# A fifth transpose for the twin rows of four tiles, a VectorE copy for the first K part, and a reversed wait list

## The chip, the cores and the metric

The kernel runs on one core of one Trainium2 chip. The metric is device time in microseconds (us) of one launch, as the median over several executions. A profiled execution gives, besides, a span (first to last recorded instruction) and a trace of every instruction.

## What is computed

A block of 2048 tokens with width 448 is normalised (layer norm without weights), then goes two ways that are multiplied and added back to the input:

```python
xn = layernorm(x)                               # x: 2048 x 448, bf16
# A: linear attention, 16 heads of 28
q, k, v = split(xn @ wqkv)
phi = lambda t: where(t > 0, t + 1, exp(t)) + 1e-6
kv = einsum("hsd,hse->hde", phi(k), v);  z = phi(k).sum over s
s = (phi(q) @ kv / (phi(q) @ z + 1e-6)) @ wo
# B: dense layer with a squared relu
h = relu(xn @ w1 + b1) ** 2                     # width 1792
g = silu(h @ w2 + b2)
out = x + s * g
```

## The kernel before, in words

**Tiles.** The tokens are cut into 16 tiles of 128 (`si`), four tiles make a group (`g`). For every tile VectorE takes the statistics (L465, L466), ScalarE makes the reciprocal deviation with a Ln and an Exp (L475, L479), and VectorE writes the normalised tile `xn` (L488). The products with `wqkv` and `w1` contract over the 448 columns, so `xn` has to be transposed into `xT`: three full chunks of 128 columns, and a rest of 64 columns.

**The rest and its twin.** The fourth chunk of `xT` holds the rest twice: rows 0 to 63 and rows 64 to 127 are the same 64 columns. The matmuls of the rest use 64 rows only, and two of them, one on each half of the array, run side by side (`half[0]`, `half[1]`). So both halves need the data. Before the change the twin is made ahead of the transpose: for tiles 0 to 3 `ln_last` (L508 to L519) writes the 64 normalised columns twice into `xn[:, si, 384:512]` with one VectorE instruction on an input that is read twice, and a transpose of 128 columns then gives both halves. From tile 4 on a small copy (`ln_twin`, L503) doubles the columns and a DMA makes the whole transpose (L551).

**The head.** Tiles 0 to 3 are transposed by TensorE instead (`pe_transpose`, L521 to L546). Tiles 0 and 1 go in two parts: part 0 is chunks 0 and 1, part 1 is chunks 2 and 3. Tiles 2 and 3 go in one part of four chunks. All transposes of a part land in one PSUM bank (`b`) and are copied to `xT` by the engine that `turn` names. Of part 0 of tile 0 each chunk has its own copy, so that the first K matmul can start after the first (`xT00a`). TensorE's order in the head is the order of the calls in L1069 to L1109: eight matmuls that only warm the array, the transposes `turn(0,0)`, `turn(0,1)`, `turn(1,0)`, then the K product of tile 0 in three parts (`mains(k0, ...)`), `turn(1,1)`, the K product of tile 1, the first halves of four `h` tiles (`h_mains`, 256 tokens), between them the transposes of tiles 2 and 3, and the rests (`rests`, 64-row matmuls). After that come the streams of K, Q and h matmuls of all groups (`pe_four`, `quads`), the products with `w2` (L957), the attention's folding, and the finish (L993, L1002) with the stores.

**What sets the order.** TensorE and the queue on SyncE keep the order in which the operations were added. For VectorE, ScalarE and GpSimd a planner in `schedule` (L88 to L229) chooses by planned durations; in the head two lists written out by hand (L1110 to L1117) fix the order on VectorE and ScalarE. PSUM banks are given out by the planner too. `emit` (L231 to L287) then works out for each operation which semaphores it must see. It goes through the operations that this one depends on from the one that the planner ends last to the one that it ends first, leaves out what is already implied, and keeps the list in that order (L258 to L268); L275 and L276 issue the waits in the order of the list.

```python
            for d in sorted(deps, key=lambda d: -d.end):
...
                need.append((d.sem, d.seq))
...
            waits[op] = need
```

In the built program an instruction holds one wait itself. Where the list has more, the instruction holds the first of the list, and the others stand ahead of it as wait instructions of their own, with one or two waits each; the trace calls these EVENT_SEMAPHORE, at L276.

Of the kernel before, what the change touches and what calls it, by code (L numbers as in the profile page):

```python
# [9 lines left out]
P = 128  # L10
# [45 lines left out]
class Program:  # L56
# [174 lines left out]
    def emit(self, nc, es):  # L231
        sems = {e: es.enter_context(nc.semaphore("q_" + e)) for e in self.ENGINES}
        clock = {}
        count = dict.fromkeys(self.ENGINES, 0)
        n_dma = 0
        last = {o for o in self.ops if o.nbytes and o.writes[0][0] == "out" and not o.succ}
        landed = es.enter_context(nc.semaphore("landed"))
        for e in self.ENGINES:
            k = 0
            for op in self.order[e]:  # L240
                if op in last:
                    op.sem, op.seq, op.key = landed, 16, ("out", op)
                elif op.nbytes:
                    op.sem, op.seq, op.key = es.enter_context(nc.semaphore(f"d{n_dma}")), 16, ("d", n_dma)
                    n_dma += 1
                else:
                    k += 1
                    op.sem, op.seq, op.key = sems[e], k, e
        done = {}
        waits = {}  # L250
        prev = {}
        for op in sorted(self.ops, key=lambda o: (o.start, 0 if o.eng == "pe" else 1)):
            e = op.eng
            known = dict(prev.get(e, {}))
            need = []
            deps = set(op.deps) | set(self.bankdeps.get(op, ()))
            deps.discard(op)
            for d in sorted(deps, key=lambda d: -d.end):  # L258
                if d.key == e == "pe" and d not in op.sync:
                    continue  # L260
                if known.get(d.key, 0) >= d.seq:
                    continue
                need.append((d.sem, d.seq))
                for kk, vv in done[d].items():
                    if known.get(kk, 0) < vv:
                        known[kk] = vv
                known[d.key] = max(known.get(d.key, 0), d.seq)
            waits[op] = need  # L268
            prev[e] = known
            done[op] = known  # L270

        def body_of(e):
            def body(h):
                for op in self.order[e]:
                    for s, v in waits[op]:  # L275
                        h.wait_ge(s, v)  # L276
                    op.emit(h, e).then_inc(op.sem, 16 if op.nbytes else 1)
                if e == "sp":
                    h.wait_ge(landed, 16 * len(last))

            return body

        body_of("pool")(nc.gpsimd)
        body_of("sp")(nc.sync)
        body_of("act")(nc.scalar)
        body_of("pe")(nc.tensor)
        body_of("dve")(nc.vector)  # L287


def bass_recurrent_scan__linear_attn_block__dense_activation_squared_relu__prompt_kernel(  # L290
# [4 lines left out]
    with ExitStack() as es:  # L295
# [186 lines left out]
            )  # L482

        def ln_norm(si, part=None):
            c = (slice(0, D if si > 3 else 384), slice(0, 256), slice(256, 384))[0 if part is None else part + 1]
            return add(
                "dve",
                lambda e, _: e.tensor_scalar(  # L488
                    out=xn[:, si, c], in0=x_tok[:, si, c], scalar1=mv[:, si, 0:1],
                    scalar2=rstd[:, si : si + 1], op0=ALU.subtract, op1=ALU.mult,  # L490
                ),
                [("x", si), ("mv", si), ("rstd", si)], [("xn", si) if part is None else ("xn", si, part)],
                0.4 if part is None else (0.22, 0.18)[part],
            )

        xn_of = lambda si: [("xn", si, 0), ("xn", si, 1)] if si < 2 else [("xn", si)]
# [8 lines left out]
                0.1 + 0.03 * (hi - lo) if eng == "dve" else 0.4,  # L505
            )

        def ln_last(si):  # L508

            x = x_tok[:, si, 384:448]  # L510
            x = bass.AP(tensor=x.tensor, offset=x.offset, ap=[x.ap[0], [0, 2], x.ap[1]])
            return add(
                "dve",
                lambda e, _: e.tensor_scalar(
                    out=xn[:, si, 384:512].rearrange("p (i c) -> p i c", i=2), in0=x, scalar1=mv[:, si, 0:1],
                    scalar2=rstd[:, si : si + 1], op0=ALU.subtract, op1=ALU.mult,
                ),
                [("x", si), ("mv", si), ("rstd", si)], [("xd", si)], 0.18,
            )  # L519

        def pe_transpose(si, part, eng):  # L521


            b = Buf("T")
            chunks = range(4) if part is None else (2 * part, 2 * part + 1)
            for i, c in enumerate(chunks):
                reads = xn_of(si)[c // 2 :][:1] or xn_of(si) if c < 3 else [("xd", si)]
                add(
                    "pe",
                    lambda e, _, i=i, c=c: e.transpose(  # L530
                        ps(b)[:, i * 64 : (i + 1) * 64].bitcast(bf), xn[:, si, c * P : (c + 1) * P], ident[:, :]
                    ),
                    reads + ["ident"] + ([b] if i else []), [b], 0.1,
                )
            def ev(e, _, lo=0, n=len(chunks)):
                src = ps(b)[:, lo * 64 : (lo + n) * 64].bitcast(bf).rearrange("p (c k) -> p c k", c=n)
                dst = xT[:, chunks[0] + lo : chunks[0] + lo + n, si * P : (si + 1) * P]
                if eng == "dve":
                    return e.tensor_copy(dst, src)
                return e.activation(out=dst, in_=src, func=AF.Copy)  # L540

            names = [("xT", si, j) for j in ((0, 1) if part is None else (part,))]
            if (si, part) == (0, 0):
                head["xT00a"] = add(eng, lambda e, x: ev(e, x, 0, 1), [b], [("xT", 0, "a")], 0.25)
                return add(eng, lambda e, x: ev(e, x, 1, 1), [b], names, 0.25)
            return add(eng, ev, [b], names, (0.42 if eng == "dve" else 0.6) if part is None else 0.25 if eng == "dve" else 0.35)  # L546

# [168 lines left out]
        def token_sum(c):  # L716

            b = Buf("A")

            def f(e, _):  # L720
                last = None
                for si in range(NT):
                    if c < 3:
                        last = e.matmul(  # L724
                            ps(b)[:, 0:D], xn[:, si, c * P : (c + 1) * P], pk_of(si), start=(si == 0),
                            stop=(si == NT - 1),
                        )
                    else:
                        r = slice(64 * (si % 2), 64 * (si % 2) + 64)
                        last = e.matmul(  # L730
                            ps(b)[r, 0:D], xn[:, si, 384:448], pk_of(si), start=(si < 2), stop=(si >= NT - 2)
                        )
                return last

            add(
                "pe", f, [("pk", i) for i in range(NT)] + [n for i in range(NT) for n in xn_of(i) + [("xd", i)]], [b], (16 if c < 3 else 8) * MM(D) + 0.1
            )

            def ev(e, eng):
                if eng == "dve":  # L740
                    return e.tensor_copy(at[:, c, :], ps(b)[:, 0:D])
                return e.activation(out=at[:, c, :], in_=ps(b)[:, 0:D], func=AF.Copy)

            add("dve", ev, [b], [("at", c)], 0.63, alts=[("act", 0.55)])
# [304 lines left out]
        for i in range(4):  # L1049
            head[f"st{i}"], head[f"mv{i}"] = ln_stats(i)  # L1050
            head[f"ln{i}"], head[f"ex{i}"] = ln_rstd(i, i + 1)
            for j in (0, 1) if i < 2 else (None,):
                head[f"xn{i}" + ("" if j is None else str(j))] = ln_norm(i, j)
            twin = head[f"xd{i}"] = ln_last(i)
        for op in masks:
            op.after = [twin]

        def warm(n, wide=False, after=()):
            b = Buf("W")
# [14 lines left out]
        def turn(si, part, eng):  # L1074
            head[f"xT{si}{part}"] = pe_transpose(si, part, eng)
# [4 lines left out]

        turn(0, 0, "act")
        turn(0, 1, "act")
        turn(1, 0, "act")
        mains(k0, (0,), [("xT", 0, "a")] + wnames("wk")[:1])
        mains(k0, (1,), [("xT", 0, 0)])
        mains(k0, (2,), [("xT", 0, 1)])
        turn(1, 1, "act")
        mains(k1, (0, 1), [("xT", 1, 0)] + wnames("wk")[:1])
        h_mains(0, (0, 1))
        mains(k1, (2,), [("xT", 1, 1)])  # L1090
# [5 lines left out]
        )  # L1096
        h_mains(0, (2,))
        h_mains(1)
        h_mains(2)
        head["xT2"] = pe_transpose(2, None, "act")  # L1100
        h_mains(3)
        head["xT3"] = pe_transpose(3, None, "dve")
        n = len(pr.ops)
        rests(k0, k1)
        k0.out()
# [2 lines left out]
        rests(first[0], first[2])  # L1108
        rests(first[1], first[3])  # L1109
        for eng, names in (  # L1110
            ("dve", "st0 mv0 st1 mv1 xn00 xn01 xd0 xn10 xn11 xd1 st2 mv2 st3 mv3 xd2 xn2 xd3 xn3 xT3"),
            ("act", "ln0 ex0 ln1 ex1 xT00a xT00 xT01 xT10 xT11 ln2 ex2 ln3 ex3 b1 xT2"),
        ):
            ops = [head[n] for n in names.split()]
            for i, op in enumerate(ops):
# [132 lines left out]
```

## Time and profile before

| | |
|---|---|
| median of 4 runs | 141.27 us (141.20 to 141.64) |
| the profiled execution | 141.34 us, span 139.70 us |
| TensorE matmuls | 136.4 us busy, 98% of the span |
| VectorE, ScalarE, GpSimd busy | 92.3, 77.9, 25.0 us |
| head: first transpose on TensorE | 4.31 us from the span's start |
| head: transposes on TensorE (L530) | 16 |
| head: last of the rests starts | 9.07 us |

The time of a run is longer than the span by 1.64 us in the profiled execution; this is start and end that no instruction covers. In the rows below, a row of the timeline gives start, duration, engine, line, operation, output and inputs; for a matmul the array shape that it uses stands ahead of the operand's shape (`128*128` is the whole array, `64*128` one of two row halves, `128*64` one of two column halves). Matmuls overlap: a row's duration is longer than the distance to the next.

### The profile page before, as it was taken

To read this page: it belongs to the slowest core of one execution; us is meant where nothing else is said; L and a number is where in the kernel's file an instruction comes from. 1 tells how busy PE (TensorE), PEld (TensorE's weight loads), DVE (VectorE), ACT (ScalarE), POOL (GpSimd) and SP (SyncE) were. 2 spreads that over 40 slices of the span, in tenths; PEclk is the share of its full clock that TensorE was granted. 3 is DMA by queue.
4 is the path that set the end of the run, shared out by engine and by line. 5 is a ranking of instruction groups with operands and counts; after the bars stand their busy time and mean duration, and the time that the engine had idled before them with its cause. 6 is when DMAs were issued, how large, how long until landed. Compare 5 with 4: busy or idle time off the path is not lost.

```text
span 139.7 us, 3098 instructions
## 1 busy us (share of the span) xinstructions
PE 136.4 (98%) x1255; PEld 68.1 (49%) x1255; DVE 92.3 (66%) x226; ACT 77.9 (56%) x152; POOL 25.0 (18%) x33
## 2 busy tenths in 40 slices
PE   9899999999999999999999999999999999999993
PEld 2474444444444444444455455645555555555482
DVE  3989889798878995889995900219836072452743
ACT  4769787869988888979788912513033030300220
POOL 6000000000000000000893000000001429092670
PEclk9999999999999999999999999999999999999999
DMA  6996379999722300000000048960000102112132
GB/s 193 242 344 202 55 188 179 359 288 151 130 52 56 66 14 0 0 19 5 0 0 0 33 114 180 175 110 0 0 0 5 66 0 99 37 62 70 37 99 66
DMA packets 20353, 12.90 MB, mean 92 GB/s; under 512 B 9524, under 2 KB 19956, under 8 KB 20340
## 3 DMA queue, kind: packets, MB, share of 16 engines
q1 hardware_dynamic: 18332, 11.52, 33.4%
q10 hardware_dynamic: 2008, 1.20, 4.4%
q8 instruction: 10, 0.16, 0.5%
q14 instruction: 3, 0.02, 0.1%
HBM read 8.78 MB, written 2.10 MB: 78 GB/s over the span
## 4 chain that ended last, share of the span: by engine, by line
PE 95%; DMA 2%; DVE 2%; issue 0%; DVEq 0%
PE pb L957 31%; PE pb L690 30%; PE pb L643 9%; PE pb L1023 8%; PE pb L724 7%; PE pb L674 6%; DMA x_tok<-in_A_x_dram 2%; PE pb L730 1%; PE pb L530 1%; DVE st L465 1%; PE pb L817 1%; PE pb L778 1%; PE pb L855 0%; DVE xn L993 0%; DVE mv L466 0%; PE pb L848 0%
## 5 line engine op out<-in xcount | busy, mean ns | idle before, releaser
L690 PE MATMUL pb<-xT,w 64*128 64x512 bf16 (+2 forms) x408 | 51.6, 365 | 0.0
L957 PE MATMUL pb<-w,r 64*128 64x448 bf16 (+3 forms) x406 | 44.9, 343 | 0.0
L699 ACT ACTIVATE r<-pb,b1f 128x512 bf16<-128x512 f32 x56 | 35.2, 689 | 4.1 <-PE pb L690 4.1
L690 PEld LDWEIGHTS pb<-xT,w 64*128 64x128 bf16 (+1 forms) x408 | 22.8, 94 | 22.5 <-ACT r L699 0.5
L957 PEld LDWEIGHTS pb<-w,r 64*128 64x128 bf16 (+1 forms) x406 | 22.9, 95 | 19.8 <-issue 0.7
L968 DVE TENSOR_TENSOR gbuf<-pb,b2b 128x448 bf16<-128x448 f32 (+1 forms) x16 | 9.2, 608 | 29.7 <-PE pb L957 29.7
L933 ACT ACTIVATE gbuf<-gbuf 128x448 bf16<-128x448 bf16 (+1 forms) x16 | 8.7, 565 | 36.0 <-DVE gbuf L968 35.5
L1002 POOL TENSOR_TENSOR xn<-xn,x_tok 128x448 bf16<-128x448 bf16 x15 | 15.1, 1034 | 46.3 <-DVE xn L993 46.3
L643 PE MATMUL pb<-w_qkv,xT 64*128 64x512 bf16 (+1 forms) x106 | 17.8, 376 | 0.0
L674 PE MATMUL pb<-xT,w_qkv 64*128 64x512 bf16 x84 | 15.5, 376 | 0.0
L707 DVE TENSOR_TENSOR r<-r 128x512 bf16<-128x512 bf16 x42 | 14.4, 416 | 0.0
L392 POOL MEMSET kvm<- 128x2048 bf16 x1 | 1.8, 1805 | 63.6 <-DVE zb L668 63.6
L1023 PE MATMUL pb<-msb,pqT 64*128 64x448 bf16 (+3 forms) x93 | 10.9, 343 | 0.0
L465 DVE BATCH_NORM_STATS2 st<-x_tok 128x6 f32<-128x448 bf16 x16 | 9.3, 609 | 2.3 <-DMA x_tok<-in_A_x_dram 2.3
L631 DVE SCALAR_TENSOR_TENSOR qk<-pb,qk 128x512 bf16<-128x512 f32 x16 | 10.6, 684 | 0.2
L993 DVE TENSOR_TENSOR xn<-pb,gbuf 128x448 bf16<-128x448 f32 (+2 forms) x17 | 9.2, 590 | 2.0 <-ACT gbuf L933 1.5
L621 ACT ACTIVATE qk<-pb 128x512 bf16<-128x512 f32 x16 | 8.9, 593 | 3.0 <-PE pb L643 2.4
L643 PEld LDWEIGHTS pb<-w_qkv,xT 64*128 64x128 bf16 (+1 forms) x106 | 6.6, 94 | 6.1 <-DMA xT<-xn 0.3
L724 PE MATMUL pb<-qk,xn 128*128 128x448 bf16 x48 | 9.3, 353 | 0.0
L621 ACT ACTIVATE pqT<-pb 128x512 bf16<-128x512 f32 x12 | 6.8, 597 | 3.1 <-PE pb L690 1.6
L674 PEld LDWEIGHTS pb<-xT,w_qkv 64*128 64x128 bf16 x84 | 6.0, 94 | 5.0
L708 ACT ACTIVATE r<-r 128x512 bf16<-128x512 bf16 x14 | 8.4, 637 | 0.0
(71 smaller groups left out, 99.7 us busy)
## 6 DMA issues: line engine op xcount, KB each, us to landing
out_dram<-xn SPq DMA_DIRECT2D x15, 112.0 KB, 1.7
w<-in_B_w_dram SPq DMA_DIRECT2D x1, 1568.0 KB, 9.9
x_tok<-in_A_x_dram SPq DMA_DIRECT2D x3, 448.0 KB, 3.8
xT<-rows ACTq DMA_DIRECT2D x6, 112.0 KB
w<-in_B_w_dram SPq DMA_DIRECT2D x1, 576.0 KB, 5.6
xT<-rows SPq DMA_DIRECT2D x5, 112.0 KB
w_o<-in_A_wo_dram SPq DMA_DIRECT2D x1, 392.0 KB, 11.1
w_qkv<-in_A_wqkv_dram SPq DMA_DIRECT2D x1, 384.0 KB, 4.1
```

The lines of the kernel that those rows point to most:

```text
L465: add("dve", lambda e, _: e.bn_stats(st6[:, si, :], x_tok[:, si, :]), [("x", si)], [("st", si)], 0.58),
L621: add("act", lambda e, _: e.activation(out=slot, in_=src(), func=AF.Exp), [buf, "actw"], [tile], 0.6)
L631: lambda e, _: e.scalar_tensor_tensor(out=slot, in0=src(), scalar=1.0 + 1e-6, in1=slot, op0=ALU.add, op1=ALU.max),
L643: return e.matmul(ps(b)[:, 0:512], xT[half[h], c, si * P : (si + 1) * P], w_qkv[half[h], c, 384 : 2 * D], start=start, stop=stop,)
L674: return e.matmul(ps(b)[:, 0:512], w_qkv[half[h], c, m * P : (m + 1) * P], xT[half[h], c, g * 512 : (g + 1) * 512], start=start, stop=stop,)
L690: return e.matmul(ps(b)[:, c0 : c0 + n], w_1[half[h], c, fi * P : (fi + 1) * P], xT[half[h], c, t : t + n], start=start, stop=stop,)
L699: lambda e, _: e.activation(out=slot, in_=ps(b)[:, 0:512], func=AF.Relu, bias=b1f[:, fi : fi + 1]),
L707: return e.tensor_tensor(out=slot, in0=slot, in1=slot, op=ALU.mult)
L724: last = e.matmul(ps(b)[:, 0:D], xn[:, si, c * P : (c + 1) * P], pk_of(si), start=(si == 0), stop=(si == NT - 1),)
L957: return e.matmul(ps(b)[:, 0:n], r2[half[h], fi, si * P : (si + 1) * P], w_2[half[h], fi, c], start=start, stop=stop)
L1002: eng, lambda e, _: e.tensor_tensor(out=ob, in0=ob, in1=x_tok[:, si, c], op=ALU.add),
L1023: return e.matmul(ps(b)[:, 0:n], q, m, start=start, stop=stop)
```

## The change

There are three parts.

1. **Twin rows from a fifth transpose.** For tiles 0 to 3 `ln_last` is gone, and the normalising instruction writes all 448 columns (in parts: 256 and 192). The fourth slot in PSUM is now filled by two transposes: one of the 128 columns 320 to 447, whose lower half is the twin, and then one of the 64 columns 384 to 447, which overwrites the upper half. So there are 20 transposes instead of 16.
2. **The first K part from VectorE.** The first chunk of tile 0 gets a PSUM bank of its own (`two`) and is copied by VectorE, not ScalarE. Part 1 of tile 1 is copied by VectorE too. The first K matmul is moved ahead of `turn(1,0)`, `turn(1,1)` ahead of the third K part of tile 0, and the transposes of tiles 2 and 3 each ahead of one `h_mains`. The lists for VectorE and ScalarE follow.
3. **The wait list is reversed** for every operation of the kernel.

```diff
-            waits[op] = need
+            waits[op] = need[::-1]
...
-            c = (slice(0, D if si > 3 else 384), slice(0, 256), slice(256, 384))[0 if part is None else part + 1]
+            c = (slice(0, D), slice(0, 256), slice(256, D))[0 if part is None else part + 1]
...
-        def ln_last(si):
...
-            b = Buf("T")
+            b, two = Buf("T"), Buf("T")
             chunks = range(4) if part is None else (2 * part, 2 * part + 1)
-            for i, c in enumerate(chunks):
-                reads = xn_of(si)[c // 2 :][:1] or xn_of(si) if c < 3 else [("xd", si)]
+            pieces = [(i, c * P, P) for i, c in enumerate(chunks) if c < 3]
+            if part != 0:
+                pieces += [(len(pieces), D - P, P), (len(pieces), 384, 64)]
+            for i, c, n in pieces:
+                reads = xn_of(si)[c // 256 :][:1] or xn_of(si)
+                o = two if (si, part, i) == (0, 0, 0) else b
                 add(
                     "pe",
-                    lambda e, _, i=i, c=c: e.transpose(
-                        ps(b)[:, i * 64 : (i + 1) * 64].bitcast(bf), xn[:, si, c * P : (c + 1) * P], ident[:, :]
+                    lambda e, _, i=i, c=c, n=n, o=o: e.transpose(
+                        ps(o)[0:n, i * 64 : (i + 1) * 64].bitcast(bf), xn[:, si, c : c + n], ident[:, :]
                     ),
...
-                head["xT00a"] = add(eng, lambda e, x: ev(e, x, 0, 1), [b], [("xT", 0, "a")], 0.25)
+                head["xT00a"] = add("dve", lambda e, x: ev(e, x, 0, 1), [two], [("xT", 0, "a")], 0.15)
...
         turn(0, 0, "act")
         turn(0, 1, "act")
+        mains(k0, (0,), [("xT", 0, "a")] + wnames("wk")[:1])
         turn(1, 0, "act")
-        mains(k0, (0,), [("xT", 0, "a")] + wnames("wk")[:1])
         mains(k0, (1,), [("xT", 0, 0)])
+        turn(1, 1, "dve")
         mains(k0, (2,), [("xT", 0, 1)])
-        turn(1, 1, "act")
         mains(k1, (0, 1), [("xT", 1, 0)] + wnames("wk")[:1])
...
+        head["xT2"] = pe_transpose(2, None, "act")
         h_mains(2)
-        head["xT2"] = pe_transpose(2, None, "act")
+        head["xT3"] = pe_transpose(3, None, "dve")
         h_mains(3)
-        head["xT3"] = pe_transpose(3, None, "dve")
...
-            ("dve", "st0 mv0 st1 mv1 xn00 xn01 xd0 xn10 xn11 xd1 st2 mv2 st3 mv3 xd2 xn2 xd3 xn3 xT3"),
-            ("act", "ln0 ex0 ln1 ex1 xT00a xT00 xT01 xT10 xT11 ln2 ex2 ln3 ex3 b1 xT2"),
+            ("dve", "st0 mv0 st1 mv1 xn00 xn01 xT00a xn10 xn11 st2 mv2 xT11 st3 mv3 xn2 xn3 xT3"),
+            ("act", "ln0 ex0 ln1 ex1 xT00 xT01 xT10 ln2 ex2 ln3 ex3 b1 xT2"),
```

## The prediction on record

> **What bounds the kernel.** I read the page's busy table and slices first, then the chain that ended last, then the waits of the head, then the timeline in narrow stretches for single starts.
>
> ```profile
> PE 136.4 (98%) x1255; PEld 68.1 (49%) x1255; DVE 92.3 (66%) x226; ACT 77.9 (56%) x152; POOL 25.0 (18%) x33
> ...
> PE   9899999999999999999999999999999999999993
> ...
> PEclk9999999999999999999999999999999999999999
> ```
>
> TensorE is full in all slices but the second and the last, at full clock. So what counts is when TensorE's stream gets going (the head), what is added to the stream, and the tail behind it. The chain in the head:
>
> ```profile
> 3.84 0.18 DVE mv L466
> 4.03 0.24 DVE xn L488
> 4.27 0.04 issue
> 4.31 0.68 PE pb L530 x4
> 4.99 0.04 issue
> 5.03 0.29 PE pb L530 x2
> 5.31 0.65 PE pb L643 x3
> ...
> 8.87 1.13 PE pb L690 x17
> ```
>
> Until 5.03 VectorE's norms set the pace; from there the chain is TensorE alone. Single starts give TensorE's idle time from the first transpose on: 0.10 before 4.54 (waits for the second norm part), 0.17 before 4.76 (the doubled rest, L514), 0.21 before 5.03 (tile 1's first part), 0.14 before 9.07 (the copy of tile 3, ended 9.01). Together 0.62 us. From 9.07 to the tail no idle time but changes of array shape is left, so this is all that a better head can win.
>
> **TensorE's prices.** Transposes follow each other in 0.056 us, 512-column matmuls in 0.216, 256-column ones in 0.109. The rows I lean on most are those where the array's shape changes:
>
> ```profile
> 8.16 0.39 PE L530 MATMUL pb<-ident,xn 128*128 128x128 bf16 x4
> 8.48 0.39 PE L643 MATMUL pb<-w_qkv,xT 64*128 64x512 bf16 x2
> ```
> ```profile
> 76.91 0.82 PE L855 MATMUL pb<-pqT,zsb 128*32 128x512 bf16 x12
> 77.66 0.55 PE L724 MATMUL pb<-qk,xn 128*128 128x448 bf16 x2
> ```
>
> Four transposes from 8.16 are through at 8.39, yet the next matmul starts at 8.48, though its data had landed at 7.23: 0.095 lost. Twelve matmuls in four column strips from 76.91 are three rounds of 0.216, through at 77.56; the next starts at 77.66: 0.10. All six changes of shape in the trace (also 74.92, 76.68, 94.29, 130.15) lose 0.09 to 0.10. In the built program the fifth transpose, with 64 columns, has the shape 128*64, its neighbours 128*128. So each of the four costs 0.056 plus two changes of 0.093: 0.24 us. The bounds of a change: 0, if a whole array takes 64 columns like the 112 of L778, which lose nothing; 0.10, the dearest row. I take 0.093: L754 and L730 are 128*64 rows.
>
> The Trainium skill ("TensorEngine Tiling (Array Packing)", Tiling Modes) says the same in words, that changing the mode drains TensorE, and speaks against this edit; without the drain four more transposes would be 0.22. The skill's "TensorE: Matmul & The Clock Gate" (Part 4) has a transpose at about 275 ns in a kernel, which would make the four 1.1 us; here the row's 0.056 decides.
>
> **The reversed waits.** Before, an instruction holds the wait that the planner ends last, and the others stand ahead of it. The built program after has it the other way round: the late one stands ahead as a wait instruction, the early one is on the instruction. So the edit does the opposite of its words. What a late wait instruction costs:
>
> ```profile
> 136.97 0.33 ACT L933 ACTIVATE gbuf<-pb 128x192 bf16<-128x192 f32 x1 [0.80 <-PE pb L956]
> 137.37 0.36 DVE L993 TENSOR_TENSOR xn<-pb,gbuf 128x192 bf16<-128x192 f32 x1 [0.41 <-ACT gbuf L933]
> ```
> ```profile
> L276 PEldq EVENT_SEMAPHORE  x51: 51/51/569, 1.2 to 100.2; - x51
> L276 DVEq EVENT_SEMAPHORE  x28: 21/36/1095, 69.2 to 137.3; - x28
> ```
>
> VectorE's last wait instruction starts at 137.305 and its multiply at 137.370: 0.065. On TensorE's queue one lasts 0.051, and two in a row stand 0.11 apart. A wait on the instruction itself takes 0.05 from a norm's end to the weight load (4.257 to 4.309), so the extra is 0.04 to 0.095; I take 0.07. It can't be a gain where the late one is really last. It is hidden wherever the signal is early: of TensorE's multi-wait groups behind 9.07 nearly all have 0.3 to 2 us of slack; the thin ones come below.
>
> **The head, step by step.** The first Ln waits 0.07 more, but VectorE is busy with tile 1's statistics until 3.94, so the first norm starts at 3.96 (3.94). First transpose: 4.28 + 0.05 + 0.07, at 4.40 (4.31). Its result is copied by VectorE 0.04 after its end (4.63): a copy 128x128 from PSUM is not in the trace; bounds 0.195 (L503, SBUF) and 0.277 (ScalarE's, L540), taken 0.22 between L503 and the 0.42 of four times the width (L539). It ends at 4.89, and the first K matmul, behind a wait instruction, starts at 5.02 (5.15). The five transposes of tile 0 and their changes of shape are done by 4.93, so the first two changes cost nothing. From 5.02 TensorE is the bound, if nothing comes late:
>
> - K starts earlier: −0.13.
> - Tile 1's first two transposes now lie behind it: +0.11.
> - Fifth transposes of tiles 1, 2, 3: 3 x 0.056 = +0.17.
> - Six changes of shape around them: 6 x 0.093 = +0.56.
> - The gap before 9.07 goes: −0.14. Tile 3's copy (from 8.86, 0.42) lets the rests go at 9.40; TensorE gets there at 9.61.
>
> Sum +0.57. What could be late: tile 1's norm starts 0.19 later behind the new copy (4.81) and ends 5.14; its transposes can go at 5.19, TensorE is free at 5.23. Tile 2's norm: statistics at 5.30 (data landed 5.17), the new copy of tile 1's part (256 columns, 0.29 between 0.22 and 0.42) at 6.05, tile 3's statistics 6.26, norm 6.99 to 7.38; transposes can go at 7.43, TensorE arrives at 7.49. Tile 3's norm hangs on ScalarE's Exp, 7.67 to 8.06: 8.12 against 8.28. Behind the copy of tile 1's part in VectorE's queue stand tile 3's statistics and both norms; it waits for a transpose that ends at 5.99, so it holds them by its own length alone. Behind the first K matmul stand tile 1's transposes, which have to wait for their norm until 5.19 anyway. The four L514 (0.22 each) that VectorE loses buy nothing, since TensorE is then last; the wider norms (0.01 to 0.02 each) hide too. ScalarE loses two copies (0.28, 0.38), also hidden. SyncE's and GpSimd's orders don't change, nor do DMAs.
>
> **Behind the head.** The planner reorders VectorE (statistics of tiles 8 and 9 go ahead of a Q evacuation, L631); that bank is free at some 22.9 + shift against a need at 23.6 + shift, hidden. Thin spots: tile 6's K product (22.69) starts 0.09 after its transposing DMA (landed 22.605), anchored to TensorE itself through the Q phase of 16.2, and the wait on this DMA now stands ahead: +0.06. Two h products (32.62, 47.73) start 0.13 after ScalarE's release: 0 to 0.02, taken 0. **Tail:** the last multiply had its wait instruction on TensorE (end 137.26) and now has it on ScalarE's silu (137.30): +0.03.
>
> **Sum:** 0.57 + 0.06 + 0.03 = +0.66, say +0.65. Against the profiled execution: span 139.70 to 140.35, time 141.34 to 141.99. The median of the runs shown is 0.07 lower: 141.27 to **141.9**.
>
> **Rivals.**
> 1. *Changing shape is free* (not slower). For: L778 and L817 use 112 columns or rows without loss. Against: six rows of six with a smaller shape lose 0.09. Then TensorE waits 0.20 for norms instead (at tile 1's copies 0.05, tile 2 0.08, tile 3 0.07): −0.13 + 0.11 + 0.17 + 0.20 − 0.14 = +0.21, with the rest +0.30: 141.55. If late wait instructions cost 0.04 as well, 141.45. It decides for not slower as soon as a change is under 0.055 us. Chance 0.2.
> 2. *A new wait behind the head.* The reordered evacuation, or tile 6's DMA (3.9 us from issue to landing, 0.03 to spare), comes late: 0.3 to 0.5 more, 142.3. For: that slack. Against: the next thinnest are over 0.1. Chance 0.13.
> 3. *The waits do what they say* (the list's last on the instruction): without the 0.07s, −0.14 at the first K, −0.06, −0.03: 141.7. Against: the built program. It lies within the forecast's range.
> 4. *Faster.* Free changes, wait instructions at 0.04, a copy of 0.195 and norms that come 0.2 early would all be needed to fill the 0.62 of idle time; less 0.22 for the transposes, −0.40: 140.9. Chance 0.06.
>
> **Chances and range.** The forecast has 0.61, spread 141.6 to 142.15: the unknown copy moves it by −0.03 to +0.06, wait instructions by −0.1 to +0.08, a change of shape by 6 x 0.01, and norms late by 0.1 cost 0.04. A measurement of this kernel tells about 0.3% from no change, 0.42 us, so up to 141.69 is no change. Slower: 0.53 of the forecast, rival 2, 0.01 of rival 1: 0.67. Same: 0.08 + 0.19: 0.27. Faster: 0.06. The range takes in rival 1 and most of rival 2: 141.4 to 142.4.
>
> **What would show it.** First transpose 4.40; first K 5.02; TensorE losing 0.09 on each side of a 64-column transpose; no wait for norms from 5.2 on; last rests at 9.6; the same distance from there to the tail but for 0.06 at tile 6. Wrong if five transposes follow each other in 0.056, if TensorE waits for VectorE at tiles 2 and 3, or if a gap appears behind 10.

## The result, and the profile after

| | before | after |
|---|---|---|
| median of the runs, us | 141.34 (63 runs, 141.05 to 142.99) | 142.40 (42 runs, 141.81 to 144.47) |
| ratio | | 1.008, 95% interval 1.0063 to 1.0098 |
| span of the profiled execution | 139.7 | 140.3 |
| norm's end to first transpose | 0.056 | 0.146 |
| first transpose to first rest | 4.17, and 0.14 idle behind it | 4.89, no idle behind it |
| first rest to the end, without that 0.14 | 131.04 | 131.11 |

The change makes the kernel slower, as forecast, but by 1.06 us instead of 0.65. The median hides how: the 42 times are two groups with nothing between them, **23 from 141.81 to 142.50 (median 142.0) and 19 from 143.64 to 144.47**. Of the 63 runs of before one is long (142.99). The ratio and its interval are of the fast runs alone, which leaves out the 11 slowest (from 144.04 on) and keeps 8 other long ones; the two medians stand at 1.0075. With 19 of 42 long, the median is among the slowest of the first group. The profiled execution, 142.00 us, belongs to the first group, and this is how its head looks (page of the changed kernel, busy times and TensorE's slices, then its timeline on TensorE):

```profile
PE 136.8 (98%) x1259; PEld 71.7 (51%) x1259; DVE 92.0 (66%) x224; ACT 77.7 (55%) x150; POOL 25.0 (18%) x33
...
PE   9799999999999999999999999999999999999993
```
```profile
4.28 0.61 PE L521 MATMUL pb<-ident,xn 128*128 128x128 bf16 x5 [0.73 <-DVE xn L488]
4.90 0.38 PE L634 MATMUL pb<-w_qkv,xT 128*128 128x512 bf16 x1
...
5.44 0.45 PE L521 MATMUL pb<-ident,xn 128*128 128x128 bf16 x3
5.82 0.82 PE L634 MATMUL pb<-w_qkv,xT 128*128 128x512 bf16 x3
6.48 0.38 PE L681 MATMUL pb<-xT,w 128*128 128x256 bf16 x2
...
7.41 0.56 PE L521 MATMUL pb<-ident,xn 128*128 128x128 bf16 x5
7.90 0.50 PE L681 MATMUL pb<-xT,w 128*128 128x256 bf16 x3
8.24 0.56 PE L521 MATMUL pb<-ident,xn 128*128 128x128 bf16 x5
8.73 0.50 PE L681 MATMUL pb<-xT,w 128*128 128x256 bf16 x3
9.16 0.39 PE L634 MATMUL pb<-w_qkv,xT 64*128 64x512 bf16 x2
```

Read it by starts. Five transposes take TensorE from 7.41 to 7.90, 0.49, where the four of before had 7.60 to 7.83, 0.23 (timeline of the kernel before, on TensorE):

```profile
7.60 0.40 PE L530 MATMUL pb<-ident,xn 128*128 128x128 bf16 x4
7.83 0.49 PE L690 MATMUL pb<-xT,w 128*128 128x256 bf16 x3
```

The 0.26 more are one transpose and two changes of array shape. From 4.90 on there is no wait for another engine. (The code is shorter after the change: the transposes are L521, K is L634, h is L681.) This page has no row for the granted clock, so the clock is read from the spacing of the matmuls. Three 512-column matmuls from 5.82 to 6.48 stand 0.22 apart, which is full clock.

VectorE's copies and the tail (timeline of the changed kernel, VectorE and ScalarE):

```profile
4.53 0.23 DVE L530 COPY xT<-pb 128x128 bf16<-128x128 bf16 x1 [0.16 <-PE pb L521]
...
5.92 0.29 DVE L530 COPY xT<-pb 128x256 bf16<-128x256 bf16 x1
```
```profile
137.55 0.33 ACT L924 ACTIVATE gbuf<-pb 128x192 bf16<-128x192 f32 x1 [0.80 <-PE pb L947]
137.98 0.36 DVE L984 TENSOR_TENSOR xn<-pb,gbuf 128x192 bf16<-128x192 f32 x1 [0.35 <-ACT gbuf L924]
```

The copies take 0.23 and 0.29, as forecast (0.22 and 0.29). In the tail ScalarE's start to VectorE's start is 0.43 against 0.40 of before: the wait instruction on the late signal costs its 0.03.

### The profile page after: what moved, and what is told of

Its sections match the earlier page's. It is cut to its first block, busy times and chain, and to the rows that moved or that the text cites. A ratio compares the mean times of both kernels' runs of the same rounds, so it can differ in the third digit from the quotient of the medians.

```text
span 140.3 us, 3100 instructions
## 1 busy us (share of the span) xinstructions
PE 136.8 (98%) x1259; PEld 71.7 (51%) x1259; DVE 92.0 (66%) x224; ACT 77.7 (55%) x150; POOL 25.0 (18%) x33
## 4 chain that ended last, share of the span: by engine, by line
PE 95%; DVE 2%; DMA 2%; ACT 0%; issue 0%; DVEq 0%
PE pb L948 30%; PE pb L681 30%; PE pb L634 9%; PE pb L1014 7%; PE pb L715 7%; PE pb L665 6%; DMA x_tok<-in_A_x_dram 2%; PE pb L521 1%; PE pb L721 1%; DVE st L465 1%; PE pb L808 1%; PE pb L769 1%; PE pb L846 0%; DVE xn L984 0%; DVE mv L466 0%; ACT gbuf L924 0%
## 5 line engine op out<-in xcount | busy, mean ns | idle before, releaser
L681 PE MATMUL pb<-xT,w 64*128 64x512 bf16 (+2 forms) x408 | 51.8, 365 | 0.0
L681 PEld LDWEIGHTS pb<-xT,w 64*128 64x128 bf16 (+1 forms) x408 | 24.4, 94 | 20.6 <-DVE pqT L615 0.3
L634 PE MATMUL pb<-w_qkv,xT 64*128 64x512 bf16 (+1 forms) x106 | 18.1, 376 | 0.0
L634 PEld LDWEIGHTS pb<-w_qkv,xT 64*128 64x128 bf16 (+1 forms) x106 | 7.0, 94 | 5.6 <-issue 0.2
```

Source lines behind the costliest of these rows:

```text
L634: return e.matmul(ps(b)[:, 0:512], xT[half[h], c, si * P : (si + 1) * P], w_qkv[half[h], c, 384 : 2 * D], start=start, stop=stop,)
L681: return e.matmul(ps(b)[:, c0 : c0 + n], w_1[half[h], c, fi * P : (fi + 1) * P], xT[half[h], c, t : t + n], start=start, stop=stop,)
```

## The two theories

The first group is the forecast: its median 142.0, against 141.9. What moved the median is the second group, so the question is what makes an execution 1.9 us longer.

**Theory A, the clock.** TensorE starts at half clock and gets the full one after a stretch of enough work. In long executions that comes late, because the idle time between the warm-up matmuls and the first transposes lies in such a stretch. **Theory B, a stall.** The clock has nothing to do with it; a wait behind the head, or one made by the reversed lists, comes late in some executions.

Half clock can be seen in the warm-up of every trace: its 512-column matmuls start 0.427 apart, where those of the stream stand 0.216 apart. For 128 columns the two distances are 0.107 and 0.056.

## Experiments

Times are medians over the runs of one call; "long" is over 143 us for the changed kernel and its parts, and over 142.4 for the kernel before, whose other runs end lower. Some expectations speak of 18 long runs in the result; the list has 19. Kernels that ran together share a chip; there were four such groups: the first four kernels below, the four on the warm-up with nine and seven, the three of the last part with the third run of the change, and the last three runs of the change.

### The change again, and its parts

The changed kernel unchanged:

> The changed kernel once more. Its 42 executions fall into two groups: 24 with spans of 140.3 to 140.8 us and 18 with 142.1 to 142.8, 1.9 us apart with nothing between; the one profile at hand is of the short group. Theory A (late clock): in the long group the array gets its full clock later, so that matmuls of 512 columns stand about 0.43 us apart instead of 0.216 for some 3 to 4 us somewhere in the first 10 us; 3.4 us at half rate cost about 1.7. Theory B (a stall behind the head): the long group has one idle stretch of TensorE of over 1 us behind 10 us from the start, at a transposing DMA or a bank. If this run's profile is of the long group it decides. Times: both groups again, about 4 in 10 at 143.6 to 144.5.

Measured: 142.05 (1 of 12 long) against 141.26, ratio 1.0069 (1.0043 to 1.0095). The first group stands where it stood. The share of long ones, 1 in 12 where 4 in 10 were expected, is smaller on this chip, and the profiled execution was a short one, so this run decides nothing between the theories.

The reversed lists alone, on the kernel before:

```diff
-            waits[op] = need
+            waits[op] = need[::-1]
```

> The kernel before with the reversed wait list alone. By the sizes measured in the changed kernel's trace (first transpose 0.146 us after its norm instead of 0.056; tile 6 or 7's K product and the tail some 0.05 each): +0.1 to +0.2 us, 141.45 to 141.55. Theory A: hardly any long executions (below 1 in 10), since the array's work in the first 8 us stays as it was but for 0.09. If the reversed waits are what makes the long group (a form of theory B), 3 or more in 10 are 1.5 to 2.5 us longer.

Measured: 141.45, ratio 1.0015 (1.000 to 1.003), none of 12 long. In its trace the first transpose comes 0.146 after the norm's end, as in the changed kernel, against 0.056. So a late wait instruction on TensorE costs 0.09; the prediction had 0.07.

The changed kernel with the old order of the lists:

```diff
-            waits[op] = need[::-1]
+            waits[op] = need
```

> The changed kernel with the wait list in its old order. Short group 0.15 to 0.25 us below the changed kernel's: 141.75 to 141.85. Theory A: the long group stays, 2 to 5 in 10, since the transposes and idle stretches ahead of 5 us stay. If the reversed waits make the long group, it is gone.

Measured: 141.72, ratio 1.0035 (1.0021 to 1.0049), none of 12 long. The first transpose is back at 0.057 behind the norm. The prediction's third rival gave 141.7 for waits that keep the late signal on the instruction. That no run was long goes against what theory A expected here, 2 to 5 in 10.

The changed kernel with the doubled norm columns of before (`ln_last`) instead of fifth transposes (the main lines of the edit):

```diff
-                pieces += [(len(pieces), D - P, P), (len(pieces), 384, 64)]
+            pieces = [(i, c * P, P) for i, c in enumerate(chunks)]
...
+            head[f"xd{i}"] = ln_last(i)
```

> The changed kernel with the doubled norm columns (one VectorE instruction for each of tiles 0 to 3) in place of the fifth transposes; order, copies and reversed waits as changed. By the prediction's prices the fifth transposes behind the first K matmul cost 0.17 + 0.56 and VectorE gets its four instructions of 0.22 back, of which two lie ahead of the norms of tiles 2 and 3: short group 0.3 to 0.6 us below the changed kernel's, 141.4 to 141.7. Theory A leaves the share of long executions open here (it depends on what the gate counts): about the same if idle time ahead of 5 us makes it, gone if the four 64-column transposes do.

Measured: 141.98, 3 of 10 long (143.12 to 143.43). A miss: no gain at all. Its trace shows why the number says little about the transposes: the clock was half for part of the head. Its first K matmuls and the transposes between them start at 4.854, 5.236, 5.343, 5.449 and 5.876: 0.38 to 0.43 for 512 columns, 0.107 for 128. From 5.95 on they are at 0.056 and 0.216. It is not the clock alone: TensorE then waits 0.21 and 0.15 for the norms of tiles 2 and 3. So the clock does change with the execution, and the head's edits can't be priced while it changes so late.

### The warm-up: nine, eight, seven matmuls

```diff
-        warm(8, wide=True)
+        warm(9, wide=True)
```

Nine on the changed kernel, on the kernel before and on the variant without fifth transposes; seven on the kernel before.

> The changed kernel with nine 512-column warm-up matmuls instead of eight (the ninth fills 0.2 to 0.43 us of the idle time between the last of them, through at 3.55, and the first transpose at 4.28). Theory A (the long executions, 1.9 us above the others, are those in which TensorE's clock stays or falls to half for one stretch of the head, because too much of some stretch is idle; in the changed kernel the first transposes come 0.09 later, so more executions fall on the wrong side): the long group shrinks or goes, at most 1 in 10 above 143.0; the short group stays at 141.8 to 142.5, median 142.05. Theory B (a stall somewhere behind the head makes the long group, the clock has nothing to do with it): 2 to 4 in 10 above 143.0 as in the changed kernel (18 of 42).

> The kernel before with seven warm-up matmuls instead of eight, and nothing else. They are through 0.2 to 0.43 us earlier. Theory A (clock): a second group appears in the kernel before as well, 1.5 to 2 us above the first, in 3 in 10 executions or more; if the profiled one is of this group, its 512-column matmuls of the head follow each other in 0.43 instead of 0.216 for some 3 us. Theory B (not the clock): as the kernel before, 141.3, at most 1 in 20 long.

> The kernel before with nine warm-up matmuls. Theory A: no long execution at all; the short group unmoved at 141.1 to 141.7 (the ninth ends by 3.95 at half clock, before the first transpose at 4.31). Theory B: the same median, a rare long one as in the kernel before (3 of 97). The median tells whether the ninth costs anything: 0 to 0.1.

> The changed kernel's order, VectorE copy and waits, with the doubled norm columns of before in place of the fifth transposes, and nine warm-up matmuls. Theory A: with the clock full in the whole head, the price of the fifth transposes shows: shape changes and transposes of tiles 1 to 3 gone (-0.73), against waits for the norms at tiles 2 and 3 that come back (+0.2 to +0.4): 141.4 to 141.75, and no execution above 143. Theory B: as without the ninth, 141.98 with 3 in 10 above 143.

Measured: the changed kernel with nine 141.94, none of 6 long, highest 142.63. The kernel before with nine 141.23 (140.96 to 141.69), ratio 0.9996 (0.9982 to 1.0011): the ninth costs nothing. The variant without fifth transposes, with nine: 141.78, none of 6, just above what was expected. With nine, 4 of the 18 runs of the changed kernel (a second call stands below) still lie at 142.58 to 142.77; none of these was traced. And the kernel before with seven, and nothing else changed, falls into two groups itself: 4 runs from 141.03 to 141.40 and 8 from 142.42 to 143.23, where the 23 runs with eight in the same call end at 141.85. The profiled one, 142.42, is of the upper group (its timeline on TensorE):

```profile
2.84 0.63 PE L1064 MATMUL pb<-ones 128*128 128x512 bf16 x1
4.27 1.11 PE L530 MATMUL pb<-ident,xn 128*128 128x128 bf16 x6 [0.80 <-DVE xn L488]
5.17 1.48 PE L643 MATMUL pb<-w_qkv,xT 128*128 128x512 bf16 x3
6.46 0.42 PE L530 MATMUL pb<-ident,xn 128*128 128x128 bf16 x2
6.67 1.06 PE L643 MATMUL pb<-w_qkv,xT 128*128 128x512 bf16 x2
7.52 0.45 PE L690 MATMUL pb<-xT,w 128*128 128x256 bf16 x2
7.81 0.38 PE L643 MATMUL pb<-w_qkv,xT 128*128 128x512 bf16 x1
```

Compare with the rows of the prediction's fences and of after: three K matmuls take 5.17 to 6.46, 0.43 each; 0.65 in all in the others. The half clock lasts to some 7.6 (to 7.66 by the record that the next section reads). Theory A stands: a second group is made in the kernel before by taking away one warm-up matmul, with none of the change's edits.

### A long execution of the changed kernel

To see the thing itself, the changed kernel ran twice more, and with seven and with nine.

> The changed kernel once more, eight warm-up matmuls, beside the three with nine on one chip. Theory A (clock): a short group at 141.8 to 142.5 and some executions 1.5 to 2 us above it (18 of 42 and 1 of 12 so far); if the profiled one is of these, 512-column matmuls of the head stand 0.43 apart for one stretch of 3 us or more, longer than in any of the short group. The kernels with nine in the same call have none.

> The changed kernel, eight warm-up matmuls, on the same chip as the two others of this call. Theory A: short group 141.8 to 142.5, long ones at 143.5 to 144.5 in any share from 5 to 45%. Theory B: the same; this run is the reference for the two beside it.

> The changed kernel with nine warm-up matmuls again. Theory A: none above 143.0, median 141.9 to 142.0. Theory B: as many long ones as after_fourth.

> The changed kernel with seven warm-up matmuls. Theory A (clock): half the executions or more lie 1.4 to 2 us above the short group (before_w7: 8 of 12), and if the profiled one is of these, its 512-column matmuls of the head stand 0.43 apart to beyond 7 us, where after_third, at the upper end of the short group, had them 0.43 apart to 6.08 only. Theory B (a stall behind the head, clock full): 43% long at most, and a gap behind 10 in a long profile.

| changed kernel with | long runs | highest of the others |
|---|---|---|
| seven warm-up matmuls | 7 of 12 | 142.24 |
| eight (four calls: 19 of 42, 1 of 12, 0 of 4, 2 of 11) | 22 of 69 | 142.61 |
| nine (two calls) | 0 of 18 | 142.77 |

The medians were 142.49 (third), 142.12 (fourth), 141.98 (nine, second time, ratio 1.0055, 1.0034 to 1.0076) and 143.55 (seven). On the chip of the last call eight gave 2 long of 11 and nine 0 of 12, which by itself is few; seven gave 7 of 12 there. All kernels with nine together have none in 51 runs. The expectation for seven was met in the share, but its profiled execution was a short one. The fourth run's profiled execution was long, 144.04 us, span 142.6. Its timeline on TensorE:

```profile
4.35 0.83 PE L521 MATMUL pb<-ident,xn 128*128 128x128 bf16 x5 [0.45 <-DVE xn L488]
5.11 0.61 PE L634 MATMUL pb<-w_qkv,xT 128*128 128x512 bf16 x1
...
6.75 1.46 PE L634 MATMUL pb<-w_qkv,xT 128*128 128x512 bf16 x3
8.01 0.64 PE L681 MATMUL pb<-xT,w 128*128 128x256 bf16 x2
8.43 0.64 PE L634 MATMUL pb<-w_qkv,xT 128*128 128x512 bf16 x1
...
9.70 0.56 PE L521 MATMUL pb<-ident,xn 128*128 128x128 bf16 x5
10.19 0.50 PE L681 MATMUL pb<-xT,w 128*128 128x256 bf16 x3
...
11.45 0.39 PE L634 MATMUL pb<-w_qkv,xT 64*128 64x512 bf16 x2
```

The program is the same as in the result's section; only the clock differs. The page's row of granted clock, and the table by stretches (length, then busy time and count of each engine, then the granted clock), do not show it:

```profile
PEclk9999999999999999999999999999999999999999
```
```profile
7.00:8.00 1.00, 1.00 (x3) 0.30 (x2) 0.97 (x4) 0.07 (x1) 0.00 (x0) 1.00 0.93 365
```

From 7 to 8 TensorE is busy all the time at a granted clock of 1.00, and yet only 3 matmuls lie in this stretch in whole or in part, where the short execution has 12. The count tells, not the clock's column. In the timeline three K matmuls take 1.26 to the next start instead of 0.66, and 256-column ones stand 0.21 apart instead of 0.11, up to 9.4. From 9.70 on the rows are those of the short execution: five transposes in 0.49. The rests start at 11.45 instead of 9.16, 2.29 later: the first K matmul starts 0.21 later (5.11 against 4.90), and from there to the first transpose of tile 2 the same work takes 4.58 instead of 2.51. From the first rest to the end the two are alike, 131.10 and 131.11. So the whole difference lies in the head, and theory B falls.

Why the column reads 1.00 can be seen in the trace itself. It holds the changes of the granted clock as records, and the page and the table take a stretch ahead of the first record as full. Here the first record is the change to full clock, at 9.557, where the matmuls change their spacing. In the kernel before with seven it stands at 7.661; in the nine other traces that have such records, all of short executions, it stands between 3.31 and 4.99. From there the full clock is recorded for 133.12 us in the first two and for 136.53 us in each of the nine. These are 39 and 40 times 3.413, so in these executions the clock changes in steps of 3.413 us, and where the steps fall differs from one execution to the next.

The third run's profiled execution (142.55, the upper end of the first group) has no such records. By its spacing it lies between (its timeline on TensorE):

```profile
4.27 0.83 PE L521 MATMUL pb<-ident,xn 128*128 128x128 bf16 x5 [0.37 <-DVE xn L488]
5.04 0.61 PE L634 MATMUL pb<-w_qkv,xT 128*128 128x512 bf16 x1
...
6.49 0.82 PE L634 MATMUL pb<-w_qkv,xT 128*128 128x512 bf16 x3
```

K stands at 0.43 to 6.08 and at full clock from there; the span is 140.9, the rests start at 9.83. So the change comes at about 6.1 in one execution and at 9.557 in the other, about one step later, and no time of the 69 lies between the two groups. In the long execution a step also ended at about 6.14 (9.557 less 3.413), without a change. What differs ahead of it is small: the first transpose came at 4.35 instead of 4.27, and TensorE was idle, as recorded, for 0.45 us instead of 0.37.

The Trainium skill ("TensorE: Matmul & The Clock Gate", Part 1) describes this: half rate as the state at rest, full rate after one busy window of some 3.4 us, and windows that run free, so that the moment depends on where the kernel's start falls in one. The 0.427, the 0.216 and the 3.413 agree. Its section on oscillation speaks of idle gaps longer than 3.4 us as the danger; here an execution with 0.45 us of idle time as recorded (from the last warm-up row's end, 3.90, to 4.35) missed a window. Idle time alone does not make a long execution: the profiled one of the change with seven was idle for 0.87 us and was short, since its clock changed at 4.03, within the gap. How much of a window may be idle these runs don't show.

### The parts, with nine warm-up matmuls

With nine warm-up matmuls no run was long, and the parts can be priced better. The ninth does not fix the clock: in the trace of *only the order* the first K matmul still takes 0.29 to the next start, in that of the variant without fifth transposes 0.38, instead of 0.216; what that loses is less than TensorE waits for VectorE further on. Three more kernels were run: only the fifth transposes, in the order and with the waits of before; only the order and the VectorE copies, with doubled columns and old waits; and the changed kernel whose fifth transpose has 128 columns, so that no shape changes (it leaves out the right columns for one half of the twin, so it is for the time alone):

```diff
-                pieces += [(len(pieces), D - P, P), (len(pieces), 384, 64)]
+                pieces += [(len(pieces), D - P, P), (len(pieces), D - P, P)]
```

> The kernel before with nine warm-up matmuls and the fifth transposes alone: the doubled norm columns go, the order, the copies on ScalarE and the waits stay as before. My price list: TensorE pays three more transposes and the changes of array shape behind its first K matmul (0.17 + 0.6), and gets back the 0.17 before 4.76 and part of the 0.21 before 5.03 for which it waited on VectorE's doubled columns: +0.4 to +0.6 on before_w9's 141.23, so 141.65 to 141.8. Rival (a fifth transpose costs little in the sum, because it takes the place of a wait for the doubled columns each time): 141.2 to 141.4.

> The changed order of TensorE and the two VectorE copies, with the doubled norm columns of before and the old order of waits, nine warm-up matmuls: no_fifth_w9 without the reversed waits. Late wait instructions at 0.05 to 0.09 a place: 0.2 to 0.3 less than no_fifth_w9's 141.78, so 141.5 to 141.6, still 0.3 above before_w9, since VectorE with both copies and the doubled columns makes TensorE wait at tiles 2 and 3 (0.28 and 0.15 in no_fifth_w9). Rival (the waits are all of it): 141.25.

> The changed kernel with nine warm-up matmuls, whose fifth transpose takes 128 columns instead of 64 (columns 320 to 448 once more), so that no array shape changes around it; the twin's upper 64 rows then hold other columns of x than the reference needs. Price of a change as in the trace of the changed kernel (0.093 in, 0.12 out): 0.65 less work on TensorE for tiles 1 to 3, of which tile 1's is eaten by the wait for tile 2's norm (its transposes start at the norm's end plus 0.15 already) and half of tile 2's by tile 3's: 0.3 to 0.4 less than after_w9's 141.94, so 141.55 to 141.65. Rival (the spacing of 0.15 is no cost of the shape but of the fifth transpose as such, another wait or its weights): no change, 141.9.

| kernel | median, us | first transpose to first rest, and idle time behind it |
|---|---|---|
| before, nine | 141.23 | 4.17 + 0.14 = 4.31 |
| only fifth transposes | 142.02 | 4.88 + 0.14 = 5.02 |
| only order and copies | 141.63 | 4.84 |
| the change, nine | 141.94 | 4.89 |
| the change, fifth with 128 columns | 141.67 | 4.41 |

The first and the fourth row ran on one chip, the others on another; against the kernel before with eight in the same call the ratios are 0.9996, 1.0067, 1.0042, 1.0061 and 1.0039 from the first row to the last.

*Only the fifth* costs more than was expected, 0.71 in the head: three transposes and three pairs of shape changes are 0.81, and only 0.1 of the waits for VectorE comes back. *Only the order* costs 0.53 in the head where 0.3 was expected, and for the reason expected: TensorE waits for the norms of tiles 2 and 3 behind the doubled columns, by starts 0.45 and 0.15 (its timeline; the row has 0.29 for the first, since recorded rows overlap):

```profile
6.80 0.60 PE L692 MATMUL pb<-xT,w 128*128 128x256 bf16 x4
7.69 0.40 PE L532 MATMUL pb<-ident,xn 128*128 128x128 bf16 x4 [0.29 <-DVE xn L488]
```

So the parts don't add up: both together cost 0.58. The new order and copies load VectorE, the fifth transposes unload it and load TensorE instead.

*The fifth with 128 columns* takes 0.47 off the head, more than the 0.3 to 0.4 expected of the time. The transposes of tile 2 there (timeline) take 0.29 for five, from 7.20 to 7.49, where the change takes 0.49:

```profile
7.20 0.45 PE L521 MATMUL pb<-ident,xn 128*128 128x128 bf16 x5
7.49 0.49 PE L681 MATMUL pb<-xT,w 128*128 128x256 bf16 x3
7.91 0.45 PE L521 MATMUL pb<-ident,xn 128*128 128x128 bf16 x5
```

Its median falls by 0.27 only, to just above the 141.55 to 141.65 expected. In the profiled execution (141.72) a transfer that VectorE waits for landed late, and TensorE waited behind it (timeline of VectorE and TensorE):

```profile
95.73 0.96 DVE L909 TENSOR_TENSOR pqT<-pqT,xT 128x1536 bf16<-128x1536 bf16 x1 [4.31 <-DMA xT<-rows]
...
97.48 1.31 PE L948 MATMUL pb<-w,r 64*128 64x448 bf16 x12 [0.32 <-DVE gbuf L959]
```

That work of VectorE starts anywhere from 94.3 to 96.2 in the traces of other executions, and at 97.1 in the long one. It costs only where TensorE gets there first: 0.48 here, 0.24 in the seven-matmul run of the change (start 96.09), 0.04 or less in the others. Whether it held back the four runs that were not traced, and with them the median, is not shown.

No version here beats the kernel before. The best one is the kernel before with nine warm-up matmuls, equal in its median.

## Why the prediction was right and wrong

**What failed.** "TensorE is full in all slices but the second and the last, at full clock. So what counts is when TensorE's stream gets going (the head), what is added to the stream, and the tail behind it." This took the clock's row of one profiled execution for the clock of all. The row reads 9 in every slice also where matmuls run at half (the long execution above, and the warm-up of before), because nothing is recorded ahead of the change to full clock; and when that comes differs from execution to execution, from 3.31 to 9.557 where it is on record. The prediction moved the first transposes later (4.40) and never asked what stood ahead of them: 0.3 to 0.9 us without work in the traces with seven or eight warm-up matmuls, right where the clock changes in most of the short executions. So a late clock stood in the sum at nothing. In the result 19 of 42 runs were 1.9 us longer, which the long execution traced above puts down to half clock in the head, and that lifted the median from 142.0 to 142.4. The trace of before held the hint: warm-up rows 0.427 apart, transposes 0.056.

**What held.** With nine warm-up matmuls, so without long runs, the change costs 0.6% (1.0061 and 1.0055), some 0.8 us; +0.65 was forecast. By steps, in the short execution:

- Head, +0.57 forecast with the wait instruction's 0.07 in it. Measured: 4.89 against 4.31 from first transpose to rests, +0.58, and 0.09 ahead of that, together more than forecast. The tail adds 0.07, and x, 0.18 earlier in this execution, brings the norm 0.13 earlier: 0.61, which is what the span grew by.
- Change of shape, 0.093 each. Into the 64-column transpose it is 0.093 (4.491 to 4.641 is 0.149, less 0.056), out of it 0.12 (8.553 to 8.729 is 0.176, less 0.056), so 0.64 for six instead of 0.56. That the changes cost time, against rival 1, is shown by the 128-column variant: 0.47 back.
- Late wait instruction, 0.07; it is 0.09 on TensorE. By the medians the reversed lists cost 0.2 on the kernel before (141.45 against 141.26) and 0.3 on the changed one (142.05 against 141.72); the forecast had 0.23 in all (0.14, 0.06 and 0.03).
- First K at 5.02, the rests that wait for tile 3's copy at 9.61 (the sum's own terms give 9.07 + 0.57 = 9.64). Measured 4.90 and 9.61: the norm ended 0.13 earlier, and on the way to the rests the dearer changes of shape took most of it back.
- No wait for norms at tiles 2 and 3: right, but with nothing to spare at tile 2. Its transposes start at 7.406, 0.156 after the norm's end at 7.25; 0.145 is the least from a norm's end to a first transpose behind a wait instruction in the traces.
- Rival 2, a new wait behind the head, would have given 142.3, close to the median for a wrong reason: from the rests to the end the change costs 0.07 (0.09 forecast), and there is no gap behind 10 in the trace.

**What stays open.** Why the changed kernel has so many more long runs than the kernel before (22 of 69 against 3 of 159 with eight warm-up matmuls; the longest of the 3 is 143.24). The later first transpose fits, 0.09 on top of 0.056 behind the norm, and so does the idle time around the fifth; neither is shown to be the cause, and the change without the fifth transposes had long runs too, 3 in 10. And neither the reversed lists alone nor the change without them gave a long run in 12, and on that chip the whole change gave only 1 in 12; the shares differ too much between chips (19 of 42 and 1 of 12) for such counts to separate the parts. That the warm-up ahead of the first transposes decides how often an execution is long is shown from both sides, by seven and by nine. Whether it does so by the idle time behind it or by the work in it stays open too, since a warm-up matmul changes both.

## What to carry to other kernels

Where a kernel warms TensorE up and then waits for its first data, look at how long the array idles between the two, and let the warm-up reach up to the first real matmul: the ninth matmul cost nothing in the median, and no run with it was long. Before pricing an edit in such a head, look at all the times, not at the median, and read the clock from the spacing of matmuls in the trace at hand; a row of full clock may only mean that nothing was recorded yet. And an edit that saves another engine's work by a smaller array shape on TensorE has to pay for the change of shape each time: five whole-array transposes took 0.29, with a 64-column one among them 0.49.

## What the hardware showed that was not expected

- TensorE ran at half clock to 9.55 in an execution whose record has 0.45 us idle between warm-up and first transpose, and the page's granted clock reads 1.00 all the while, since the trace's clock records begin only with the change at 9.557.
- The full clock came at about 6.1 or at 9.557 in executions of one program, one step of 3.4 us apart; the times fall into two groups, with nothing between 142.61 and 143.64 in 69 runs.
- Leaving a 64-column transpose costs more (0.12 us) than entering it (0.093 us).
- Two edits that each cost over 0.5 us alone (fifth transposes 0.71, order and copies 0.53) cost 0.58 together.
